# A convolution and gate kernel: more products of zeros at the start, and new orders for the opening and the closing

## The chip, the cores and the metric

The kernel runs on one core of a Trainium2 chip. The metric is the time of one execution on the device in microseconds (us). A core has TensorE (PE, and PEld for its weight loads), VectorE (DVE), ScalarE (ACT), GpSimd (POOL) and SyncE (SP), each with its own stream of instructions, and 16 DMA engines that they share.

## The reference

The input x has shape 8 x 4224 x 192. A causal convolution of seven taps runs along the sequence, with softmaxed weights, one set for each of eight heads of 24 channels. On its result y a gated block is computed: a causal convolution of five taps for each channel, a sigmoid, a product with y times a 192 x 192 matrix, and a second such matrix.

```python
w = exp(weight - max); w = w / (sum(w) + 1e-9)
y[b, s, h, g] = sum over k of w[h, k] * x_pad[b, s + k, h, g]
gate_pre[b, s, d] = sum over k of conv_w[k, d] * y_pad[b, s + k, d]
out = (sigmoid(gate_pre) * (y @ w_val)) @ w_out
```

## The kernel before

**Groups and steps.** The sequences lie one behind the other in two halves, the halves side by side on the partitions. They are cut into nine groups, and each group into four steps (the last into two), 34 in all, of 360 to 512 positions. The 192 channels are in three units: units 0 and 1 (tile x1, one for each half) and unit 2 (tile x2, the remaining 64 channels of both halves).

**First convolution.** `load_x` (token L) fetches a piece of x in windows, on SP's queue, into one of nine buffers. `conv_begin` (U) multiplies a set of windows by the tile `band`, which holds the softmaxed weights: in group 0 a set is 32 matmuls of 64 x 64 by 58 in f32, in the next seven groups 36. A group has six sets. Each needs two loads and two PSUM banks. `conv_end` (K) copies one bank to a tile e on ScalarE, and `scatter` (D) spreads e by DMA over x1 or x2. The eight pieces of group 0's x2 are issued by POOL (`BY_POOL`), all others by SP. Group 0's first two sets give x2, the other four x1.

**Steps.** For step n and unit i, `tap0` (Z) is ScalarE's first tap into PSUM, `tap` (T) one of four multiply-adds on VectorE, `sigmoid` (S) is ScalarE's. `cast_x` (CX, ScalarE) and `rest_x` (XL, GpSimd) split x1 or x2 into a rounded part and a remainder. The tokens V12, V21, V22, V110 and V111 are parts of the product with w_val on TensorE. `gated` (G, VectorE) multiplies it by the gate. `cast_g` and `rest_g` (CG, GL) split that, the parts O12 to O111 are the product with w_out, `evacuate` (E, ScalarE) copies it out of PSUM, and ST stores it. In the last step GL is VectorE's, and E0 too.

**Weights and zeros.** `hw`, `rwv` and `rwo` fetch the head weights and the two matrices, which come as 64-bit numbers. The steps wa, wb, wc (`decode_a`, `decode_b`, `decode_c`) turn a matrix into f32 on VectorE, wp puts it in place (wv on VectorE, wo on GpSimd), wh (`cast`, ScalarE) and wl (`rest`, VectorE) split it. mx, we, sm, bd0 and bd1 make `band`. tl and tl2 load ScalarE's tables. `warm_up` (wu) multiplies a tile of zeros by itself ten times into a bank nothing reads.

**Order.** Nothing is reordered by a scheduler: each engine executes its instructions in the order in which the tokens are written. `PROLOGUE` covers the opening, up to step 4 and parts of step 5. The loop over `window(n)` emits `SCHEDULE` for steps 5 to 17 in pairs. `EPILOGUE` covers the rest, from about step 18 to step 33, with parts of steps 15 to 17. In the token `T21.0` the unit is 2, the tap 1 and the step 0; `D0.0.5` is group 0, x1, head 5; `O110.33` is the product with w_out of unit 0 by its own rows, for step 33.

```python
with tc.manual_schedule(engines={ENG.SP, ENG.PE, ENG.Activation, ENG.DVE, ENG.Pool}):
    emit(PROLOGUE)
    for n in range(FIRST, BEHIND, 2):
        window(n)
    emit(EPILOGUE)
```

Of the kernel before, what the change touches and what calls it, by code (L numbers as in the profile page):

```python
# [112 lines left out]
L T04.0 D1.0.3 Z1.1 XL1.0 G2.1 Z0.1 G2.0 K T11.1 U K T01.1 D1.1.3 T12.1 V21.0 K D1.1.1 T02.1 K
D1.0.1 V111.0 T13.1 CG2.0 D1.1.2 V110.0 S0.0 T03.1 D1.0.2 T14.1 U CG2.1 D1.0.5 T04.1 GL2.1 Z2.2
D1.0.4 U G0.0 Z1.2 L G1.0 GL2.0 K D1.1.0 V111.1 T21.2 K T11.2 CG0.0 U D1.0.7 S0.1 T22.2 T12.2 K
V12.3 CG1.0 T23.2 CX1.2 V21.1 T13.2 GL1.0 T24.2 K V110.1 GL0.0 T14.2 D1.1.7 Z2.3 G1.1 D1.0.6 Z0.2
T21.3 O21.0 K L T01.2 K D1.1.4 V12.2 CG1.1 T22.3 D1.1.5 S2.2 T02.2 O22.0 L CX2.3 T23.3 L O110.0
XL2.3 L T03.2 O12.0 L T24.3 XL1.2 D1.1.6 T04.2 V22.3 Z0.3 G0.1 O111.0 S2.3 T01.3 CX2.2 E1.0 G2.3
# [9 lines left out]
O111.16 T22.19 CX1.18 O22.16 T01.18 CX1.19 XL1.18 O111.15 T23.19 CX2.19 T02.18 V22.18 E2.16 T24.19  # L128
O21.16 K G2.18 Z0.19 XL1.19 O21.15 D6.0.1 T03.18 E1.16 L U T01.19 S2.19 L CG2.17 T04.18 E1.15
O110.16 L T02.19 GL2.17 Z1.19 O110.15 T03.19 S0.18 V111.18 XL2.19 T11.19 E0.15 T04.19 V21.18 E0.16  # L130
ST.15 T12.19 Z1.20 L U G1.18 ST.16 CG0.17 T13.19 K V110.18 GL0.17 CG2.18 T11.20 D6.0.2 K O12.17
T14.19 CG1.17 GL2.18 V12.19 T12.20 Z2.20 G0.18 K GL1.17 V22.19 T21.20 CG0.18 D6.1.2 O22.17 T13.20 K
D6.0.3 GL0.18 O111.17 S0.19 T22.20 L V111.19 D6.1.0 G2.19 CX2.20 V110.19 T23.20 L CX1.20 D6.1.3
T14.20 V21.19 E2.17 D6.1.1 XL1.20 T24.20 O21.17 Z2.21 G1.19 Z0.20 U T21.21 CX1.21 G0.19 O110.17
XL2.20 L E1.17 T22.21 CX2.21 T01.20 V22.20 K XL1.21 T23.21 K O12.18 CG1.18 T02.20 CG1.19 V12.20
T24.21 S2.20 T03.20 V12.21 XL2.21 Z0.21 T04.20 S2.21 V22.21 E0.17 GL1.19 T01.21 O22.18 CG0.19 ST.17
G2.21 Z1.21 O110.18 L GL1.18 T02.21 E2.18 V111.20 G2.20 S0.20 O111.18 T11.21 CG2.19 T03.21 O21.18
GL2.19 T12.21 V21.20 E1.18 T04.21 E0.18 U GL0.19 G1.20 Z1.22 T13.21 V110.20 K L T11.22 D6.0.5 K U
T14.21 CG2.20 ST.18 G0.20 D6.0.4 GL2.20 Z2.22 O22.19 T12.22 L K D6.0.6 T21.22 CG0.20 O12.19 D6.0.7 K
T13.22 O12.20 L E2.19 T22.22 D6.1.4 S0.21 U T14.22 L CX2.22 T23.22 Z2.23 O111.19 XL2.22 D6.1.6  # L140
T24.22 CG1.20 V110.21 T21.23 K O22.20 GL1.20 D6.1.7 Z0.22 T22.23 V111.21 E2.20 L T01.22 GL0.20 S2.22
V21.21 T23.23 K D6.1.5 O21.19 T02.22 CX2.23 O21.20 CX1.22 T24.23 D7.0.0 T03.22 O110.19 Z0.23 XL1.22
G1.21 O111.20 E1.19 T04.22 E0.19 O110.20 E1.20 T01.23 ST.19 Z1.23 V12.22 D7.0.1 G0.21 XL2.23 CG2.21
# [5 lines left out]
CX1.25 T01.24 O21.21 D7.0.4 XL2.25 T24.25 D7.1.1 O22.22 E1.21 T02.24 L CG2.23 O110.21 GL1.22 D7.1.3
Z0.25 T03.24 V22.24 S2.25 T01.25 V110.24 K XL1.25 T04.24 CG0.23 O111.22 E0.21 T02.25 E2.22 V21.24  # L150
ST.21 G2.24 Z1.25 L O21.22 T03.25 GL0.23 CX2.26 D7.0.5 T11.25 U CG2.24 L S0.24 T04.25 GL2.23 V111.24
T12.25 Z1.26 G0.24 O110.22 K T11.26 E1.22 V22.25 D7.0.6 E0.22 T13.25 O12.23 K G1.24 CX1.26 D7.0.7
# [584 lines left out]
```

## Time and profile before

| | us |
|---|---|
| median of three runs | 366.04 |
| lowest, highest | 364.3, 367.31 |
| the profiled execution | 365.04 |
| its span, first to last instruction | 363.2 |

A group's row in the profile names the line, the engine, the operation, what it writes and reads, the shape and the count; behind the bar stand busy time, mean duration in ns, and the idle time of the engine just before, with what ended it. A row of the timeline gives start, duration, engine, line, operation and tiles; the bracket holds the idle time before it and its releaser ("issue" where no semaphore event explains it). A row of stretches gives, for each engine, busy time and number of instructions, then the granted share of TensorE's clock, the DMA share and GB/s. An f32 matmul shows as two rows of TensorE, a rounded one (fp32r) as one, and each row has a weight load.

### The profile page before, as it was taken

The page shows a single profiled execution, that of the slowest core. Times are in us where ns is not written, and L with a number is a line of the kernel's source. Part 1 is how long each engine was busy: PE and PEld are TensorE (multiplying, and loading weights), DVE is VectorE, ACT ScalarE, POOL GpSimd, SP SyncE. Part 2 cuts the span into 40 slices and gives each one's busy share as a digit, 9 for nine tenths or more (in the row PEclk, how much of TensorE's full clock was granted, in tenths as well). Part 3 has the DMA queues.
Part 4 walks back from the last instruction along what each step waited for, and adds up shares of the span by engine and source line. Part 5 has one row for each costly group of instructions (what it writes and reads, how often), then busy time and mean ns, then how long its engine had stood idle before and what let it go on. Part 6 is the DMA issues. An engine that isn't in the chain of part 4 may idle for free.

```text
span 363.2 us, 12709 instructions
## 1 busy us (share of the span) xinstructions
PE 341.8 (94%) x5184; PEld 247.0 (68%) x5184; DVE 338.7 (93%) x551; ACT 318.5 (88%) x550; POOL 242.0 (67%) x191
## 2 busy tenths in 40 slices
...
PEclk9655999999999999999999999999999999999998
...
GB/s 241 338 213 312 227 251 287 152 298 332 212 302 270 221 250 285 263 247 203 275 240 257 269 213 372 183 246 226 250 167 244 257 141 134 110 103 178 36 180 178
DMA packets 36234, 83.21 MB, mean 229 GB/s; under 512 B 4688, under 2 KB 7760, under 8 KB 36176
## 3 DMA queue, kind: packets, MB, share of 16 engines
...
q0 software_dynamic: 384, 0.95, 1.2%
q8 instruction: 41, 0.67, 0.8%
...
## 4 chain that ended last, share of the span: by engine, by line
PE 72%; DVE 13%; DMA 7%; issue 4%; ACT 3%; SPq 0%; DVEq 0%; ACTq 0%
PE pc L386 13%; PE po L553 11%; PE pv L553 11%; DVE pg L468 8%; PE po L536 7%; PE pv L536 7%; PE po L545 7%; PE pv L545 6%; PE po L561 5%; PE pv L561 5%; DMA x<-e 4%; DVE g L583 3%; DMA x<-xw 2%; DVE g L468 2%; ACT e L412 1%
## 5 line engine op out<-in xcount | busy, mean ns | idle before, releaser
L468 DVE SCALAR_TENSOR_TENSOR pg<-x,cwt,pg 128x512 f32<-128x512 f32 (+5 forms) x306 | 210.9, 732 | 4.4 <-ACT pg L458 3.9
L493 POOL TENSOR_TENSOR pl<-g,ph 128x512 fp32r<-128x512 f32 (+4 forms) x99 | 124.1, 1270 | 44.1 <-ACT ph L490 23.2
L493 POOL TENSOR_TENSOR xl<-x,xh 128x1024 fp32r<-128x1024 f32 (+8 forms) x68 | 111.8, 1661 | 54.4 <-ACT xh L490 28.9
L458 ACT ACTIVATE pg<-x,cwt 128x510 f32<-128x510 f32 (+5 forms) x102 | 70.5, 695 | 13.1 <-DVE g L468 8.6
L386 PEld LDWEIGHTS pc<-band,x 64*64 64x64 f32 x3600 | 61.3, 142 | 23.2 <-issue 12.8
L386 PE MATMUL pc<-band,x 64*64 64x58 f32 (+2 forms) x3600 | 67.0, 228 | 9.4 <-issue 8.0
L468 DVE SCALAR_TENSOR_TENSOR g<-x,cwt,pg 128x510 f32<-128x510 f32 (+5 forms) x102 | 73.3, 723 | 0.2
L583 DVE TENSOR_TENSOR g<-pv,g 128x512 f32<-128x512 f32 (+5 forms) x102 | 67.6, 667 | 2.1 <-ACT g L475 1.3
L412 ACT COPY e<-pc 128x512 f32<-128x512 f32 (+2 forms) x102 | 57.6, 591 | 11.6 <-PE pc L386 11.3
L490 ACT CAST ph<-g 128x512 fp32r<-128x512 f32 (+5 forms) x102 | 62.7, 622 | 1.2 <-PE po L545 0.6
L594 ACT COPY ot<-po 128x512 f32<-128x512 f32 (+5 forms) x101 | 56.7, 585 | 5.7 <-ACT g L475 2.3
L475 ACT ACTIVATE g<-g 128x512 f32<-128x512 f32 (+6 forms) x68 | 56.8, 836 | 2.8 <-DVE g L468 2.8
L490 ACT CAST xh<-x 128x512 fp32r<-128x512 f32 (+9 forms) x68 | 54.4, 828 | 0.1
L536 PE MATMUL pv<-x,wvf 128*64 128x256 f32 (+5 forms) x272 | 35.0, 391 | 2.3 <-DMA x<-e 2.3
L536 PE MATMUL po<-g,wof 128*64 128x256 f32 (+5 forms) x272 | 35.5, 384 | 0.0
L553 PE MATMUL pv<-xh,wvh 128*128 128x512 f32 (+5 forms) x68 | 29.3, 431 | 0.1
L536 PEld LDWEIGHTS pv<-x,wvf 128*64 128x64 f32 x272 | 19.2, 142 | 14.4 <-DMA x<-e 2.8
L553 PE MATMUL po<-ph,woh 128*128 128x510 f32 (+5 forms) x68 | 28.1, 413 | 0.5 <-ACT e L412 0.5
L553 PE MATMUL pv<-xl,wvh 128*128 128x512 f32 (+5 forms) x68 | 26.3, 386 | 0.4 <-POOL xl L493 0.4
L553 PE MATMUL pv<-xh,wvl 128*128 128x512 f32 (+5 forms) x68 | 26.2, 386 | 0.1
L553 PE MATMUL po<-ph,wol 128*128 128x510 f32 (+5 forms) x68 | 26.2, 386 | 0.0
L553 PE MATMUL po<-pl,woh 128*128 128x510 f32 (+5 forms) x68 | 26.2, 385 | 0.0
...
## 6 DMA issues: line engine op xcount, KB each, us to landing
x<-xw SPq DMA_DIRECT2D x60, 256.0 KB, 5.6
x<-e SPq DMA_DIRECT2D x56, 256.0 KB, 5.1
...
x<-e SPq DMA_DIRECT2D x8, 232.0 KB, 6.3
...
```

The source lines that it names most:

```text
L386: nc.tensor.matmul(b[r][cols, k * p.run + a : k * p.run + a + n], lhsT=t[rows, o + 64 * c : o + 64 * c + 64], rhs=band[rows, pairs[k] + (c ...
L412: nc.scalar.copy(e[:, :n], opened[g, u][r][:, :n])
L458: nc.scalar.mul(acc, unit_view(n, i, 0), cwt[:, i // 2, 0:1])
L468: nc.vector.scalar_tensor_tensor(out=dst, in0=unit_view(n, i, k), scalar=cwt[:, i // 2, k : k + 1], in1=acc, op0=ALU.mult, op1=ALU.add,)
L475: nc.scalar.activation(v, v, AF.Sigmoid)
L490: nc.scalar.copy(h, x)
L493: eng.tensor_tensor(out=l, in0=x, in1=h.bitcast(F32), op=ALU.subtract)
L536: nc.tensor.matmul(acc[p, c], lhsT=self.w.f[:, W12 : W12 + 64], rhs=self.x1[:, q, c], start=first and i == 0, stop=not first and i == 1,)
L545: nc.tensor.matmul(acc, lhsT=a[p, W21 : W21 + 128], rhs=b[p], start=first and i == 0, stop=not first and i == 2,)
L553: nc.tensor.matmul(acc, lhsT=a[:, W11 : W11 + 128], rhs=b[:, q], start=first and i == 0, stop=not first and i == 2,)
L583: nc.vector.tensor_tensor(out=v, in0=pvs.pop((n, q)), in1=v, op=ALU.mult)
L594: nc.scalar.copy(dst, pos.pop((n, q)))
```

## The change

The zeros are given in two kinds: `warm_up` can first run products on quarters of the array (64 x 64 by 58, four side by side, in two banks), then whole ones of 122 x 122. The first step runs ten rounds of quarters (40 products) and five whole ones, instead of ten whole ones. Steps wx0 to wx3 of four whole products each are added, of which the opening list uses three. The two lists are written in another order; the loop's table is the same. All lines behind `warm_up` have numbers higher by six.

```diff
-    def warm_up(n):
+    def warm_up(n, quarters=0):
 
-        t = bank("warm")
+        t = [bank(f"warm{r}") for r in range(1 + (quarters > 0))]
+        for _ in range(quarters):
+            for r, rows in enumerate(HALVES):
+                for cols in HALVES:
+                    nc.tensor.matmul(
+                        t[r][cols, :WIN], lhsT=zeros[rows, :64], rhs=zeros[rows, :WIN], start=True, stop=True
+                    )
         for _ in range(n):
-            nc.tensor.matmul(t[:122, :122], lhsT=zeros, rhs=zeros, start=True, stop=True)
+            nc.tensor.matmul(t[0][:122, :122], lhsT=zeros, rhs=zeros, start=True, stop=True)
...
 PROLOGUE = """
-hw tl msk wu rwv L L mx L L we L sm L L bd0 bd1 rwo wav L wbv L U U K L K L tl2 U L L K L wao K
+hw tl msk wu rwv L rwo mx L L we L tl2 sm L L L wx0 L wx2 wao L wx1 bd0 bd1 wbo U wav wbv U K L wcv
...
 EPILOGUE = """
...
-ST.32 O12.33 GL1.33 O110.33 E2.33 O111.33 ST2.33 E0.33 E1.33 ST0.33 ST1.33
+ST.32 O12.33 GL1.33 O21.33 E2.33 ST2.33 O111.33 E0.33 ST0.33 E1.33 ST1.33
...
-        "wu": lambda: warm_up(10), "wu2": lambda: warm_up(6), "tl": warm_exp, "msk": band_mask, "mx": maxima, "sm": sums, "L": load_x, "U": conv_begin, "K": conv_end,
+        "wu": lambda: warm_up(5, 10), "tl": warm_exp, "msk": band_mask, "mx": maxima, "sm": sums, "L": load_x, "U": conv_begin, "K": conv_end,
...
+    for i in range(4):
+        ONCE[f"wx{i}"] = lambda: warm_up(4)
```

In the opening, rwo is now the third transfer on SP's queue instead of the tenth, the first two decoding instructions of wo stand ahead of bd0 and bd1 on VectorE, and tl2 stands ahead of the first copies of e on ScalarE.

TensorE at the start of the program, before: the zeros, then the first set of group 0 (pc is its PSUM bank, x the loaded piece; the repeats between are left out).

```order
L725 UNCONDITIONAL_BRANCH
L295 MATMUL warm<-zeros 122x122 x10
L386 MATMUL pc_0_0_170<-band,x_0_137 64x58 x2
L386 MATMUL pc_0_1_171<-band,x_0_137 64x58 x2
L386 MATMUL pc_0_0_170<-band,x_0_139 64x58 x2
L386 MATMUL pc_0_1_171<-band,x_0_139 64x58 x2
```

TensorE at the same place now; the first two rows stand ten times, in turn.

```order
L297 MATMUL warm_125<-zeros 64x58 x2
L297 MATMUL warm_126<-zeros 64x58 x2
L301 MATMUL warm_125<-zeros 122x122 x5
L301 MATMUL warm_197<-zeros 122x122 x4
L301 MATMUL warm_204<-zeros 122x122 x4
L301 MATMUL warm_213<-zeros 122x122 x4
L392 MATMUL pc_0_0_222<-band,x_0_173 64x58 x2
L392 MATMUL pc_0_1_223<-band,x_0_173 64x58 x2
```

All 57 products of zeros stand ahead of the first convolution matmul, where ten did.

SP's queue around group 0's pieces of x1, before (x_0_238 is x1; rows that read `xw` are loads of x).

```order
L244 DMA x_5_283<-xw 128x512
L244 DMA x_0_285<-xw 128x640
L244 DMA x_0_289<-xw 128x512
L430 DMA x_0_238<-e_3_0_428 16x8x464
L430 DMA x_0_238<-e_2_1_301 16x8x464
L430 DMA x_0_238<-e_3_1_430 16x8x464
L430 DMA x_0_238<-e_4_1_474 16x8x464
L430 DMA x_0_238<-e_5_0_478 16x8x464
L430 DMA x_0_238<-e_4_0_433 16x8x464
L430 DMA x_0_238<-e_2_0_296 16x8x464
L430 DMA x_0_238<-e_5_1_496 16x8x464
L244 DMA x_1_508<-xw 128x640
```

SP's queue there now (x_0_294 is x1).

```order
L244 DMA x_5_346<-xw 128x512
L436 DMA x_0_294<-e_2_1_404 16x8x464
L436 DMA x_0_294<-e_3_1_444 16x8x464
L436 DMA x_0_294<-e_2_0_402 16x8x464
L436 DMA x_0_294<-e_4_1_489 16x8x464
L436 DMA x_0_294<-e_4_0_486 16x8x464
L244 DMA x_0_495<-xw 128x640
L244 DMA x_0_498<-xw 128x512
L436 DMA x_0_294<-e_3_0_441 16x8x464
L436 DMA x_0_294<-e_5_1_510 16x8x464
L436 DMA x_0_294<-e_5_0_504 16x8x464
L244 DMA x_1_527<-xw 128x640
```

The first two loads of group 1 moved from ahead of the eight pieces to behind the fifth.

TensorE at the end of the program, before: products with w_out for steps 32 and 33 (po is the bank, ph and pl the split gate product).

```order
L536 MATMUL po_2_5724<-g_32_5571,wof 64x208 x4
L545 MATMUL po_0_5754<-ph_33_5720,woh 128x360
L545 MATMUL po_1_5755<-ph_33_5720,woh 128x360
L545 MATMUL po_0_5754<-ph_33_5720,wol 128x360
L545 MATMUL po_1_5755<-ph_33_5720,wol 128x360
L545 MATMUL po_0_5754<-pl_33_5721,woh 128x360
L545 MATMUL po_1_5755<-pl_33_5721,woh 128x360
L536 MATMUL po_2_5738<-g_33_5639,wof 64x180 x4
L553 MATMUL po_0_5754<-ph_5751,woh 128x360
L553 MATMUL po_0_5754<-ph_5751,wol 128x360
L553 MATMUL po_0_5754<-pl_5752,woh 128x360
```

TensorE at the end now.

```order
L559 MATMUL po_0_5807<-ph_5798,woh 128x360
L559 MATMUL po_0_5807<-ph_5798,wol 128x360
L559 MATMUL po_0_5807<-pl_5799,woh 128x360
L542 MATMUL po_2_5801<-g_33_5683,wof 64x180 x4
L551 MATMUL po_0_5807<-ph_33_5746,woh 128x360
L551 MATMUL po_1_5818<-ph_33_5746,woh 128x360
L551 MATMUL po_0_5807<-ph_33_5746,wol 128x360
L551 MATMUL po_1_5818<-ph_33_5746,wol 128x360
L551 MATMUL po_0_5807<-pl_33_5747,woh 128x360
L551 MATMUL po_1_5818<-pl_33_5747,woh 128x360
```

For step 33, O110 (the rows that read ph_5798 and pl_5799) moved from behind O21 and O12 to ahead of both; in both programs three more rows follow, O111.

More of the change, by code (lines that the diff above doesn't have):

```diff
@@ L113 @@
[L113 to L118, printed above, removed]
@@ L124 @@
+L G1.2 V21.3 L E2.1 T12.4 GL2.2 L K U K T21.4 S0.3 XL2.4 T13.4 D2.1.1 V12.4 D2.0.2 T22.4 CG0.2 T14.4
+V110.3 T23.4 Z2.5 O12.2 G0.3 CG1.2 V111.3 T24.4 GL1.2 T21.5 Z0.4 G1.3 GL0.2 S2.4 K K D2.0.4 L L
+D2.0.1 D2.0.5 D2.0.3 L D2.0.0 L D2.1.3 D2.1.2 D2.1.0
 """
@@ L127 @@
 EPILOGUE = """
[L128 to L143, printed above, removed]
@@ L149 @@
[L149 to L152, printed above, removed]
-V12.25 T12.26 CG1.23 T14.25 U GL1.23 G2.25 Z2.26 T13.26 O22.23 K T21.26 GL2.24 CG0.24 D7.1.6 U
-T14.26 E2.23 ST.22 K XL2.26 T22.26 L V21.25 Z2.27 D7.1.4 T23.26 O21.23 K XL1.26 D7.1.7 S0.25 T21.27
@@ L179 @@
[L179 to L182 removed]
+T22.19 CX2.19 O21.16 K XL2.19 T23.19 CX1.18 O111.15 T01.18 D6.0.1 V22.18 CX1.19 T24.19 L XL1.18
+O22.16 T02.18 Z0.19 O110.15 T03.18 E2.16 O110.16 CG0.17 T01.19 O111.16 S2.19 GL0.17 T04.18 E0.16
@@ new lines @@
+O12.20 T23.23 L V12.23 CG0.20 T01.22 D7.0.0 S2.22 T24.23 GL0.20 K O21.20 T02.22 CX2.23 D7.0.1 O22.20
+Z0.23 G2.22 XL2.23 O110.19 T03.22 CG2.22 V22.23 T01.23 E2.20 GL2.22 S2.23 O110.20 T04.22 O111.19
+T02.23 XL1.23 Z1.23 O111.20 G2.23 CG0.21 T11.23 E0.20 V110.22 S0.22 T03.23 V111.22 T12.23 E1.20
+O21.19 T04.23 CG1.21 V21.22 E0.19 T13.23 GL1.21 Z1.24 U G0.22 CG2.21 T14.23 GL0.21 E1.19 V111.23
+T11.24 K ST.19 Z2.24 G1.22 GL2.21 V21.23 ST.20 S0.23 T12.24 U T21.24 CX2.24 G1.23 CX1.24 O12.21
+XL2.24 T13.24 K T22.24 V110.23 K XL1.24 D7.0.3 T14.24 O22.21 K D7.0.2 CX2.25 G0.23 O111.21 D7.1.3
@@ new lines @@
+T11.26 Z2.27 O22.23 XL1.26 T12.26 CX2.27 V110.25 E2.23 T21.27 V111.25 K T13.26 S0.25 D7.1.7 U T22.27
+D7.0.7 CX1.27 T14.26 O110.23 D7.1.6 G0.25 Z0.26 D7.1.4 V22.26 G1.25 CG0.24 D7.0.6 T01.26 O21.23
+CG1.24 L S2.26 T23.27 GL1.24 D7.1.5 O111.23 K T02.26 O22.24 D8.0.0 CG1.25 T24.27 GL0.24 V12.27
+T03.26 Z0.27 V12.26 XL2.27 T04.26 E1.23 K T01.27 O12.24 Z1.27 D8.0.1 GL1.25 T02.27 S0.26 V22.27
+T11.27 O110.24 E0.23 G2.26 E2.24 ST.23 O12.25 T12.27 S2.27 D8.0.2 CG0.25 T03.27 L O21.24 CG2.25
+T13.27 D8.0.3 V21.26 GL2.25 E0.24 T04.27 O111.24 G2.27 Z1.28 XL1.27 T14.27 V110.26 E1.24 T11.28
```

93 lines of the change are left out of this document (52 added, 41 removed).

## The prediction

> **What bounds the kernel now.** I read the page first: busy shares, the clock in the slices, the queues.
>
> ```profile
> span 363.2 us, 12709 instructions
> ...
> PE 341.8 (94%) x5184; PEld 247.0 (68%) x5184; DVE 338.7 (93%) x551; ACT 318.5 (88%) x550; POOL 242.0 (67%) x191
> ...
> PEclk9655999999999999999999999999999999999998
> ...
> q8 instruction: 41, 0.67, 0.8%
> ```
>
> Two engines are nearly full and TensorE ran at half clock early on. One queue carries instructions: 41 packets for TensorE's 5184 + 5184 = 10368 instructions, so 253 a packet. Next, busy time by stretch, cut where TensorE stops.
>
> ```profile
> 0.00:10.60 10.60, 8.71 (x222) 7.90 (x222) 3.05 (x15) 5.00 (x10) 1.63 (x12) 1.00 0.78 265
> 10.60:13.60 3.00, 0.11 (x5) 0.00 (x0) 2.35 (x6) 0.97 (x3) 3.00 (x6) 0.81 1.06 396
> 13.60:17.32 3.72, 3.68 (x127) 3.50 (x127) 3.51 (x11) 0.92 (x3) 1.13 (x3) 0.50 1.07 283
> 20.30:24.01 3.71, 3.66 (x127) 3.50 (x127) 0.56 (x1) 1.38 (x3) 0.83 (x3) 0.50 0.97 207
> ...
> 45.95:100.00 54.05, 53.02 (x772) 37.86 (x772) 53.68 (x86) 49.85 (x87) 34.80 (x26) 1.00 0.93 256
> 100.00:300.00 200.00, 199.04 (x3119) 142.33 (x3122) 198.88 (x307) 191.83 (x327) 149.04 (x105) 1.00 0.82 244
> 300.00:354.90 54.90, 54.36 (x426) 38.45 (x418) 54.32 (x90) 49.09 (x88) 42.09 (x32) 1.00 0.34 128
> ```
>
> Columns: TensorE matmuls, TensorE loads, VectorE, ScalarE, GpSimd, then clock, DMA share, GB/s. From 45.95 to 354.9 VectorE idles 0.37 + 1.12 + 0.58 = 2.1 us in 309. It sets the pace there, and a new order cannot give back more than that 2.1 us. What can be won lies before 46 us and after 354.9. The counts show the other limit: TensorE stops after 444 instructions, then after 254 more, then 254 again, about the 253 of one packet. The stops are waits for a read of instructions.
>
> ```profile
> 1.15 4.49 PE L295 MATMUL warm<-zeros 128*122 128x122 f32 x20 [1.15 <-DVE zeros L299]
> 13.64 3.68 PE L386 MATMUL pc<-band,x 64*64 64x58 f32 x127 [2.93 <-issue]
> 20.35 3.66 PE L386 MATMUL pc<-band,x 64*64 64x58 f32 x127 [3.04 <-issue]
> 25.97 0.75 PE L561 MATMUL pv<-xh,wvh 128*128 128x462 f32 x1 [1.96 <-ACT xh L490]
> 45.97 0.45 PE L386 MATMUL pc<-band,x 64*64 64x58 f32 x15 [1.32 <-issue]
> ```
>
> "issue" means that no semaphore explains the wait. From go-on to go-on: 20.35 - 13.64 = 6.7 us and 25.97 - 20.35 = 5.6 us for one packet's worth, of which the work is 3.7. Last, what VectorE waits for, and the transfers behind it:
>
> ```profile
> 10.54 4.19 POOL L430 DMA_DIRECT2D x<-e  x8 [8.10 <-ACT e L412]
> 11.18 0.36 DVE L307 TENSOR_SCALAR wo_g<-raw_wo 128x384 int32<-128x384 int32 x1 [5.32 <-DMA raw_wo<-wo]
> 15.33 0.98 DVE L338 TENSOR_TENSOR wvf<-wv_h,wv_l 128x64 f32<-128x64 f32 x5
> 17.39 8.78 SPq L430 DMA_DIRECT2D x<-e  x8
> 23.59 1.22 ACT L458 ACTIVATE pg<-x,cwt 128x464 f32<-128x464 f32 x2 [0.45 <-DMA x<-e]
> 31.33 1.22 ACT L458 ACTIVATE pg<-x,cwt 128x464 f32<-128x464 f32 x2 [3.04 <-DMA x<-e]
> 32.02 3.75 DVE L468 SCALAR_TENSOR_TENSOR pg<-x,cwt,pg 128x464 f32<-128x464 f32 x6 [2.27 <-ACT pg L458]
> 37.88 1.19 DVE L583 TENSOR_TENSOR g<-pv,g 128x462 f32<-128x462 f32 x2 [0.90 <-ACT g L475]
> 39.77 2.52 DVE L468 SCALAR_TENSOR_TENSOR pg<-x,cwt,pg 128x462 f32<-128x462 f32 x4 [0.71 <-ACT pg L458]
> ```
>
> VectorE's work on group 0 starts in earnest at 32.02, when the last of eight pieces of x1 has landed (31.33, where ScalarE's first tap goes on) plus 0.69 of that tap. After it come two waits, 0.90 + 0.71 = 1.6 us, and then it is full. So the time is: landing of x1, plus those waits, plus fixed VectorE work, plus the tail.
>
> **The change part by part.**
>
> *Zeros.* Ten products of zeros were 20 matmul rows in 4.49 us, 0.224 a row. Now there are 40 quarter products (80 rows) and 5 + 12 whole ones (34 rows). A quarter product has the shape of a convolution matmul: at half clock 127 rows in 3.68, 0.029 a row, so 2.3 us. The five: 10 x 0.224 = 2.2, to 1.15 + 4.5 = 5.7 us, about where the old zeros ended. The last 24 rows take 24 x 0.224 = 5.4 at that price and about 2.7 if the clock has doubled. TensorE reaches group 0 at 8.4 (or 11.1) where it was there at 5.6. I take 8.4: in the trace the clock reads 1.00 in the first row and the zeros before it were as dense. What covers the delay: the band now stands behind the decode of raw_wo, and nothing can start before it; with raw_wo issued ahead of the second load, it should be there near 7.6 (estimate).
>
> *Where the reads fall.* Each f32 matmul is four instructions (10 zeros, 20 rows, as many weight loads). Before, the first stop lies (444 - 40) / 4 = 101 convolution matmuls in, the next at 164.5 and 228. Now 57 products of zeros are 228 instructions: stops at (444 - 228) / 4 = 54, 117.5, 181, 244.5. Group 0 has 6 x 32 = 192, so three stops fall inside it where two did. I take the first to be covered: its read, asked for one packet ahead, is asked for among the zeros, by 5.7, and at 5.6 to 6.7 us a read it is there at 11.3 to 12.4, while TensorE gets there at 8.4 + 54 x 0.037 = 10.4 (67.0 us for 1800 convolution matmuls in the page's group, shown next). Price 0 to 2 us, taken at 0.5, since the DMA engines are less loaded at 3 us than at 13.6.
>
> ```profile
> L386 PE MATMUL pc<-band,x 64*64 64x58 f32 (+2 forms) x3600 | 67.0, 228 | 9.4 <-issue 8.0
> ...
> x<-xw SPq DMA_DIRECT2D x60, 256.0 KB, 5.6
> ...
> x<-e SPq DMA_DIRECT2D x8, 232.0 KB, 6.3
> ...
> x<-e POOLq DMA_DIRECT2D x8, 116.0 KB, 8.7
> ```
>
> The second stop comes near 13 and lasts to about 17, the third ends near 23, and the last 11 matmuls of group 0 end near 23.4. Before, they ended at 20.35 + 27.5 x 0.058 = 21.9. So TensorE itself is 1.5 us later, not earlier. What can make x1 earlier is the rest.
>
> [...] Here the first stop comes after 444 and costs 2.93 us. [...]
>
> *VectorE and ScalarE.* raw_wo is third in SP's queue, so VectorE no longer waits 5.32 us for it with wv's decode behind it. wvf was done at 15.33 + 0.98 = 16.3; now about 13.5 (7.6, then the same decode instructions: two of wo, four and five of wv at 0.36 to 0.57, and the 0.98). ScalarE's cast of wvh, which the copies behind it wait for, comes 2.8 us earlier, and with it SP's first piece of x1 (17.39, now 15).
>
> *SP.* Two loads of group 1 move from ahead of the eight pieces to behind the fifth.
>
> ```profile
> 0.00:31.33 31.33, 19.21 (x482) 16.52 (x482) 16.92 (x45) 12.94 (x25) 9.97 (x26) 0.70 0.93 268
> 14.50:23.59 9.09, 6.05 (x228) 5.87 (x223) 5.20 (x15) 3.26 (x8) 2.13 (x6) 0.50 1.05 226
> ```
>
> The DMA engines are full (share 0.93) up to x1's landing: 268 GB/s x 31.33 us = 8.4 MB. What x1 needs is 12 loads of 0.26, the two weights (0.78), eight pieces of 0.116 and eight of 0.232: 6.6 MB; with the two loads still ahead of its last pieces, 7.2 MB, or 27.0 us at that rate. That is the early end. The late end is 31.33 plus the 1.5 us by which TensorE is later: 32.8. I take 29.4, nearer the middle: the pieces start 2.4 us earlier, but the last needs TensorE at 23.4, a copy, and the 6.3 us that such a piece takes to land. Gain 1.9, between +1.5 and -4.3.
>
> *VectorE's later waits.* The first gate product is now step 0's, whose sigmoid is early, so the 0.90 goes; late next is TensorE, whose stop after 1458 instructions falls in step 1's products. I give it the 1.32 of the stop at 45.97: 1.6 becomes 1.3. Ends 0 and 2.5.
>
> *The middle and the closing list.* The loop's code is the same, its read boundaries shift. One wait of VectorE in 300 us came from TensorE (0.7, below); I take one again, between none and three. The closing list keeps the end: last taps, sigmoid, two gate products, two remainders on VectorE, then TensorE's last 24 matmul rows.
>
> ```profile
> DVE g L583 <- PE pv L545: 0.7, 1, 0.7
> ...
> 356.12 0.53 DVE L493 TENSOR_TENSOR pl<-g,ph 128x360 fp32r<-128x360 f32 x1 [0.22 <-ACT ph L490]
> 357.11 0.53 DVE L493 TENSOR_TENSOR pl<-g,ph 128x360 fp32r<-128x360 f32 x1 [0.45 <-ACT ph L490]
> ...
> 357.51 0.43 PE L553 MATMUL po<-ph,woh 128*128 128x360 f32 x1
> ```
>
> O110.33 now starts once the first remainder is there (356.65), with O12 and O21 behind it, about 1.5 us of cover for the second (357.64). It ends within 0.3 of before: 0.
>
> *Sum.* -1.9 - 0.3 + 0 + 0 = -2.2 us. The profiled execution was 365.04 (span 363.2 and 1.8 around it), which gives 362.8. The median of the runs is 366.04, 1.0 above it; on that the forecast is **363.8 us**.
>
> **Rivals.** *First, slower: the clock comes late.* If the clock has not doubled by 5.7, the zeros last to 11.1, group 0 starts 2.7 later than forecast, and x1 lands at 32.8 or later: 31.33 + 1.5 + 2.7 less what the DMA queue hides, about 34. That is +2.7 less 0.3: 368.4. It decides from a start of group 0 after about 10. For it: the row at 10.60 to 13.60 shows 0.81, the clock does fall. Against: 4.5 us of zeros sufficed once. [...] *Second: all falls into place.* x1 lands near 27 and both later waits go: -4.3 - 1.0 = -5.3, 360.7. For it: 1.2 MB of other loads were moved before x1 landed. Against: the last piece needs TensorE. *Third: no effect.* x1 lands when the DMA engines are done, at 31.3 as now, and the stops were covered by that wait: 366.0. For it: DMA share 0.93 to 1.06 all the way. *Fourth: the closing list costs VectorE.* It is full there, and four waits like the 0.7 above add 2.8: 366.6.
>
> **How the numbers follow.** Forecast 0.40, first 0.12, second 0.21, third 0.21, fourth 0.06. The forecast's own range is 362 to 365.5. For 8 in 10 the range goes from 360.4 (the second rival) to 367.9 (most of the first). A measurement of this kernel can tell about 1% from no change, that is 362.4 and 369.7. Faster: the second rival nearly whole (0.18) and a quarter of the forecast (0.10), 0.28. Slower: a third of the first and a part of the fourth, 0.07. The same: 0.65.
>
> **What would show it.** Counts by stretch: the first stop within group 0 absent or short, stops after 698 and 952 instructions of about 3 us. Zeros to 8.4, the clock at 1.00 by 6. ScalarE's first tap on x1 at 29.4 instead of 31.33, VectorE's idle time after it about 1.3 us. If x1 lands at 31 or later, or if VectorE idles over 2 us between 100 and 355, the forecast is wrong.

## The result, and the profile after

The changed kernel takes 370.40 us (median of 5 runs, 369.81 to 371.25) against 366.04 us before: a ratio of 1.0124, with a 95% interval from 1.008 to 1.0169. It is slower: both ends of the interval lie above 1. The profiled execution took 371.25 us, 6.2 more than the one before (365.04). In a second session the medians were 370.12 and 365.11 us (ratio 1.0098, 1.0042 to 1.0154).

Single executions of one kernel lie up to 9 us apart here, and the ratios use those within 1.5% of a kernel's fastest; a long wait for instructions stands in the profile of one of the others, as will be seen.

From the page of the profile after, the same rows as were shown of the page before:

```profile
span 369.3 us, 12883 instructions
...
PE 345.9 (94%) x5278; PEld 248.7 (67%) x5278; DVE 339.8 (92%) x551; ACT 319.0 (86%) x550; POOL 242.4 (66%) x191
...
PEclk9865999999998999999999999999999999999999
...
q8 instruction: 41, 0.67, 0.8%
```

VectorE's work is 339.8 us where it was 338.7, so some 5 of the 6.1 us of span are waits of VectorE; the other 1.1 us are longer instructions of its own, for which no run here shows a reason. Where the waits lie is told by its busy time by stretch; the columns are start and end, length, VectorE's busy time (instructions), granted clock, DMA share, GB/s. Before:

```profile
33.00:60.00 27.00, 25.02 (x43) 0.94 0.90 254
60.00:100.00 40.00, 40.00 (x64) 1.00 0.91 252
100.00:115.00 15.00, 15.00 (x25) 1.00 0.94 287
115.00:354.00 239.00, 237.70 (x373) 1.00 0.70 214
```

After:

```profile
33.00:60.00 27.00, 24.39 (x41) 0.90 1.05 261
60.00:100.00 40.00, 39.69 (x63) 1.00 0.89 242
100.00:115.00 15.00, 10.90 (x18) 0.89 1.01 280
115.00:354.00 239.00, 237.95 (x369) 1.00 0.70 214
```

Idle time went from 1.98 to 2.61 us in the first stretch, from 0 to 0.31 in the second, from 0 to 4.10 in the third, and from 1.30 to 1.05 in the rest: +4.8 us, of which one stretch of 15 us has 4.1. The clock there is 0.89. Ahead of 33 us VectorE idles 15.99 us where it was 15.10, and behind 354 us 5.49 where it was 6.13. The timelines of TensorE, SyncE, ScalarE and VectorE in the opening:

```profile
14.92 3.53 PE L392 MATMUL pc<-band,x 64*64 64x58 f32 x127 [2.17 <-issue]
19.55 0.57 PE L392 MATMUL pc<-band,x 64*64 64x58 f32 x22 [1.10 <-issue]
26.11 1.34 PE L392 MATMUL pc<-band,x 64*64 64x58 f32 x40 [5.99 <-DMA x<-xw]
...
19.77 1.03 SPq L244 DMA_DIRECT2D x<-xw  x2
20.85 2.70 SPq L436 DMA_DIRECT2D x<-e  x3
...
32.29 1.22 ACT L464 ACTIVATE pg<-x,cwt 128x464 f32<-128x464 f32 x2 [7.79 <-DMA x<-xw]
...
32.97 3.75 DVE L474 SCALAR_TENSOR_TENSOR pg<-x,cwt,pg 128x464 f32<-128x464 f32 x6 [6.28 <-DMA x<-xw]
```

The zeros did their work: only two stops of 2.17 and 1.10 us are left inside group 0, and its last product ends at 19.55 + 0.57 = 20.1 us. Yet VectorE's first tap on x1 starts at 32.97, 0.95 later than before: TensorE was early, and the transfers were not.

The largest loss, seen on the timelines of TensorE and, in the last row, of VectorE near 106 us:

```profile
103.02 2.31 PE L392 MATMUL pc<-band,x 64*64 64x58 f32 x144
105.26 1.08 PE L542 MATMUL po<-g,wof 128*64 128x254 f32 x8
109.07 0.50 PE L559 MATMUL pv<-xh,wvh 128*128 128x510 f32 x1 [2.73 <-DVE pg L474]
...
110.73 0.63 PE L559 MATMUL pv<-xh,wvh 128*128 128x510 f32 x1
...
113.90 0.69 DVE L589 TENSOR_TENSOR g<-pv,g 128x510 f32<-128x510 f32 x1 [4.10 <-PE pv L551]
```

Two neighbouring sets of convolution products (144 rows, with their loads 288 instructions) take 2.3 us; after eight rows of another product comes a gap of 2.73 us. The row behind it names VectorE's tap as the releaser, but the gap is a wait for instructions, as the next two views show. First, TensorE's rows in the 3 us ahead of the gap, in the gap and behind it (products, loads, VectorE, ScalarE, GpSimd, clock, DMA share, GB/s):

```profile
103.37:106.35 2.98, 2.98 (x144) 2.32 (x136) 2.98 (x5) 2.98 (x7) 2.52 (x2) 1.00 1.06 316
106.35:109.07 2.72, 0.00 (x0) 0.00 (x0) 2.72 (x6) 2.72 (x6) 2.33 (x2) 1.00 1.01 395
109.07:113.75 4.68, 4.68 (x19) 2.90 (x19) 0.73 (x2) 1.97 (x4) 3.97 (x4) 0.64 0.93 295
```

Second, the queues of the transfers in 106.5 to 107.7 us (from 103.37 to 106.5 the view has no row for the queue of instructions at all):

```profile
q1 hardware_dynamic: 94, 0.47, 98.5%
q8 instruction: 1, 0.02, 5.7%
```

So TensorE used up a block of 256 instructions (the prediction worked out 253 for a packet) in 2.98 us, the read of the next began 3.1 us after the block was entered, ran 1.1 us, and TensorE went on another 1.4 us later. Behind the gap the clock is granted at 0.64 for 4.7 us, and VectorE, whose next gate product waits for TensorE, loses 4.1 us for a gap of 2.7.

### The profile page after: what moved, and what is told of

Read it like the earlier page. It is cut to its first block, busy times and chain, and to the rows that moved or that the text cites. A ratio compares the mean times of both kernels' runs of the same rounds, so it can differ in the third digit from the quotient of the medians.

```text
span 369.3 us, 12883 instructions
## 1 busy us (share of the span) xinstructions
PE 345.9 (94%) x5278; PEld 248.7 (67%) x5278; DVE 339.8 (92%) x551; ACT 319.0 (86%) x550; POOL 242.4 (66%) x191
## 4 chain that ended last, share of the span: by engine, by line
PE 82%; DMA 10%; DVE 3%; issue 2%; ACT 1%; POOL 0%; SPq 0%; DVEq 0%; ACTq 0%
PE pc L392 14%; PE pv L559 13%; PE po L559 12%; PE po L542 8%; PE pv L542 8%; PE po L551 7%; PE pv L551 7%; PE po L567 6%; PE pv L567 6%; DMA x<-xw 6%; DMA x<-e 5%; DVE pg L474 2%; PE warm L301 1%; ACT e L418 1%; PE warm L297 1%
## 5 line engine op out<-in xcount | busy, mean ns | idle before, releaser
L499 POOL TENSOR_TENSOR xl<-x,xh 128x512 fp32r<-128x512 f32 (+7 forms) x68 | 112.2, 1663 | 68.3 <-ACT xh L496 21.6
L600 ACT COPY ot<-po 128x512 f32<-128x512 f32 (+5 forms) x101 | 57.6, 584 | 10.7 <-ACT g L481 2.9
L496 ACT CAST xh<-x 128x512 fp32r<-128x512 f32 (+7 forms) x68 | 55.2, 836 | 2.6 <-PE pv L551 2.6
```

What stands on the lines that cost most here:

```text
L496: nc.scalar.copy(h, x)
L499: eng.tensor_tensor(out=l, in0=x, in1=h.bitcast(F32), op=ALU.subtract)
L600: nc.scalar.copy(dst, pos.pop((n, q)))
```

## The experiments

Block boundaries can be counted. Number TensorE's recorded instructions from 0, its waits for semaphores and its three drains included: in every profile here the stops of this kind stand ahead of numbers 449, 705, 961 and so on, every 256th (in the kernel before at 13.63, 20.35 and 25.97 us; the gap that ends at 109.07 in the changed one stands ahead of 3777, which is 449 + 13 x 256). So instructions that are added ahead of a place, where TensorE idles anyway, move the boundaries there and are meant to move nothing else. All medians in one table (runs of one session share the runs of the kernel before; its medians were 365.1 to 366.3):

| run | from | median us (lowest to highest, runs) | ratio to before (95%) |
|---|---|---|---|
| e2_old_closing | changed | 370.33 (367.88 to 375.86, 6) | 1.0116 (1.0071 to 1.0161) |
| b_new_zeros | before | 365.07 (362.58 to 371.05, 10) | 0.9971 (0.9927 to 1.0014) |
| e4_old_zeros | changed | 374.30 (372.74 to 377.51, 4) | 1.0280 (1.0202 to 1.0359) |
| e3_loads_last | changed | 374.45 (373.38 to 379.31, 4) | 1.0250 (1.0202 to 1.0297) |
| e6_loads_first | changed | 373.60 (370.23 to 376.76, 6) | 1.0169 (1.0105 to 1.0233) |
| e1_pad128 | changed | 369.57 (367.47 to 371.68, 4) | 1.0126 (1.0066 to 1.0185) |
| e5_pad_late | changed | 375.73 (373.88 to 377.83, 4) | 1.0296 (1.0209 to 1.0382) |
| b_pad208 | before | 367.19 (366.39 to 371.20, 10) | 1.0062 (1.0013 to 1.0110) |
| b_pad64 | before | 369.42 (366.73 to 369.57, 4) | 1.0104 (1.0024 to 1.0184) |
| a_split | changed | 370.91 (369.00 to 374.66, 6) | 1.0130 (1.0071 to 1.0189) |
| bz_split | before | 366.47 (365.55 to 368.67, 12) | 1.0036 (1.0011 to 1.0061) |
| after_again | changed | 370.12 (365.24 to 374.41, 10) | 1.0098 (1.0042 to 1.0154) |
| b_new_zeros2 | before | 364.73 (363.60 to 366.56, 10) | 1.0009 (0.9978 to 1.0039) |
| e8_no_stores | changed | 365.84 (362.71 to 368.19, 10) | 1.0030 (0.9993 to 1.0068) |
| a_no_wx | changed | 364.77 (363.31 to 369.38, 12) | 0.9993 (0.9958 to 1.0029) |
| c_quarters | before | 364.41 (362.03 to 371.18, 12) | 0.9981 (0.9941 to 1.0020) |

**Which part of the change costs.** The closing list was put back:

```diff
 EPILOGUE = """
-T22.19 CX2.19 O21.16 K XL2.19 T23.19 CX1.18 O111.15 T01.18 D6.0.1 V22.18 CX1.19 T24.19 L XL1.18
+O111.16 T22.19 CX1.18 O22.16 T01.18 CX1.19 XL1.18 O111.15 T23.19 CX2.19 T02.18 V22.18 E2.16 T24.19
...
```

> The changed kernel with the closing list of before; opening list and zeros as changed. Theory (the closing list costs and gives nothing; the loss lies before 115 us): 369.5 to 371.5, the stop at 106 and VectorE's 4.0 us there as in the changed kernel. Rival (the closing list gives VectorE new waits): 366 to 368.

It took 370.33 us, with a gap of 1.59 us at 108.7 in the profiled execution (368.11), smaller than expected there: the closing list costs and gives nothing that shows. Then the zeros alone were put into the kernel before:

```diff
-hw tl msk wu rwv L L mx L L we L sm L L bd0 bd1 rwo wav L wbv L U U K L K L tl2 U L L K L wao K
+hw tl msk wu rwv L L mx L L we L sm L wx0 wx2 L wx1 bd0 bd1 rwo wav L wbv L U U K L K L tl2 U L L K L wao K
...
-        "wu": lambda: warm_up(10), "wu2": lambda: warm_up(6), "tl": warm_exp, "msk": band_mask, "mx": maxima, "sm": sums, "L": load_x, "U": conv_begin, "K": conv_end,
+        "wu": lambda: warm_up(5, 10), "tl": warm_exp, "msk": band_mask, "mx": maxima, "sm": sums, "L": load_x, "U": conv_begin, "K": conv_end,
```

> The kernel before with the changed kernel's zeros alone (first zeros in quarters and three steps of four more), its lists as before; 188 instructions more ahead of group 0. If the zeros do what they are for: no stop at the first boundary within group 0, short ones at the next two, its last product ends 1 to 2 us earlier than 24.0 and x1 lands at 29.5 to 31 instead of 31.3. The boundaries behind it move by 188: blocks nearly wholly in pairs end near 47, 104 (2.9 us of work) and 201 (2.0); stops of 1 to 3.5 us there, VectorE idle 1 to 3 us behind each of the last two. Time 365.5 to 370. Rival (zeros alone carry the change's worth, and the moved boundaries cost nothing): 363 to 365.

365.07 us, just between the two that were expected: no loss, no sure gain. The first stop of group 0 is gone, and VectorE's first tap on x1 starts at 31.44 instead of 32.02. Against e2_old_closing, which differs from it in the opening list alone, that is 5.3 us, so the loss came with the opening list. But the execution that was profiled here was a long one, 371.05 us, and its timeline has the same gap:

```profile
108.08 0.79 PE L559 MATMUL pv<-xh,wvh 128*128 128x510 f32 x1 [4.25 <-DVE pg L474]
```

The two kernels have the same boundary there, so the old list too can lose time at it. The other way round, the zeros of before in the changed lists:

```diff
-hw tl msk wu rwv L rwo mx L L we L tl2 sm L L L wx0 L wx2 wao L wx1 bd0 bd1 wbo U wav wbv U K L wcv
+hw tl msk wu rwv L rwo mx L L we L tl2 sm L L L L wao L bd0 bd1 wbo U wav wbv U K L wcv
...
-        "wu": lambda: warm_up(5, 10),
+        "wu": lambda: warm_up(10),
```

> The changed kernel's lists with the zeros of before: ten whole products, none in quarters, none of the three later steps; 188 instructions fewer ahead of group 0. If the zeros are what brings the reads of instructions forward: the first stop of 2.9 us is back inside group 0's 192 products, and group 0's last product ends at 21.5 to 23 instead of 20.1. If the landing of x1 hangs on that: it lands at 33.5 or later, time over 371; if it hangs on the queue of transfers alone: at 31.5 to 32.5, and the time is set by the blocks, which begin 188 instructions later in the code: the block near 105 still lies mostly in the pair of sets (stop of 1 to 2.5 us), time 368.5 to 371.

The first stop was back in group 0, as expected (2.52 us, with a second of 2.24), the last product of group 0 ended at 19.7 us, earlier than the 21.5 to 23 expected, and VectorE's first tap on x1 began at 32.07, so x1 did not hang on the zeros. The time, 374.30 us, was above what was expected: other blocks had stops,

```profile
88.27 1.89 PE L392 MATMUL pc<-band,x 64*64 64x58 f32 x68 [1.77 <-issue]
105.58 0.61 PE L392 MATMUL pc<-band,x 64*64 64x58 f32 x26 [0.93 <-issue]
...
243.33 0.33 PE L392 MATMUL pc<-band,x 64*64 64x48 f32 x7 [1.60 <-issue]
```

so, by this one profile, the zeros were worth more in the changed lists for where they put the boundaries than for anything they did early on.

**SyncE's two loads.** They were moved behind the last piece of x1, and in another run ahead of the first:

```diff
-D0.0.3 wpo U K D0.0.0 K D0.0.5 who D0.0.4 wlo L wlv L Z2.0 D0.0.2 T21.0 K CX2.0 T22.0 K XL2.0 T23.0
-CX2.1 D0.0.7 Z2.1 T24.0 D0.0.6 XL2.1 T21.1 S2.0
+D0.0.3 wpo U K D0.0.0 K D0.0.5 who D0.0.4 wlo wlv Z2.0 D0.0.2 T21.0 K CX2.0 T22.0 K XL2.0 T23.0
+CX2.1 D0.0.7 Z2.1 T24.0 D0.0.6 L L XL2.1 T21.1 S2.0
```

> The changed kernel with the two loads of group 1 moved on SP's queue from behind the fifth to behind the eighth piece of x1. Theory (x1 lands late because these two loads, 2.7 us in the queue, go ahead of its last three pieces): the last piece lands at 29 to 30 us instead of 32.26, VectorE's first tap on x1 starts at 30 to 31 instead of 32.97, the rest as before, time 367.5 to 369. Rival (the pieces themselves go slowly, at 150 GB/s, whatever stands ahead of them): the last lands at 31.5 to 32.5, time 370 to 371.

VectorE's first tap on x1 came 3.1 us earlier, as the theory had it, and the time rose by 4 us, which it had not. TensorE's and VectorE's timelines:

```profile
31.08 2.17 PE L392 MATMUL pc<-band,x 64*64 64x58 f32 x72 [8.63 <-DMA x<-xw]
...
29.90 3.75 DVE L474 SCALAR_TENSOR_TENSOR pg<-x,cwt,pg 128x464 f32<-128x464 f32 x6 [0.72 <-ACT pg L464]
...
41.05 3.73 DVE L474 SCALAR_TENSOR_TENSOR pg<-x,cwt,pg 128x462 f32<-128x462 f32 x6 [4.95 <-ACT pg L464]
```

Group 1's first set waits 8.63 us for its loads, and VectorE waits 4.95 us at 41, in the first taps of group 1: the queue's order says which of the two is late.

```diff
-K L U K L K D0.1.6 U D0.1.0
+K L U K L K L L D0.1.6 U D0.1.0
...
-D0.0.3 wpo U K D0.0.0 K D0.0.5 who D0.0.4 wlo L wlv L Z2.0
+D0.0.3 wpo U K D0.0.0 K D0.0.5 who D0.0.4 wlo wlv Z2.0
```

> The changed kernel with the two loads of group 1 ahead of all eight pieces of x1 on SP's queue, as the kernel before has them. Theory (the queue of transfers sets the landing of x1, and having the loads in the middle of the pieces only makes group 1's first set late): the loads land by 19 us, TensorE's wait of 5.9 us ahead of group 1's first set goes, the last piece lands at 30.5 to 32; VectorE's waits from 33 to 60 us fall from 2.6 to under 2 us; the stop near 106 stays; time 369 to 370.4. Rival (pieces land later behind two more loads): last piece at 33 or later, 371 or more.

The wait of 5.9 us went and VectorE's first tap on x1 began at 32.49, as the theory had it; the time rose to 373.60. The profiled execution, the longest of six, had longer stops (4.02 us at 23.36, 3.22 at 40.67, 2.25 at 54.76, 2.52 at 113.52). Neither place of these two loads wins back the loss.

**Moving the boundaries.** 128 instructions of zeros were put where TensorE idles:

```diff
+    ONCE["wy"] = lambda: warm_up(0, 8)
...
-CX2.1 D0.0.7 Z2.1 T24.0 D0.0.6 XL2.1 T21.1 S2.0 L L T22.1 L U T23.1
+CX2.1 D0.0.7 Z2.1 T24.0 D0.0.6 XL2.1 T21.1 S2.0 L L T22.1 L wy U T23.1
```

> The changed kernel with 32 quarter products of zeros more, 128 instructions, put where TensorE idles from 20.1 to 26.0 us, ahead of group 1's first set: every later block of 256 instructions begins 128 instructions earlier in the code, and nothing else moves. Theory (a stop comes where one block lies wholly inside two neighbouring sets of convolution products, 288 instructions that TensorE works off in 2.3 us): the block that was used up in 2.97 us and left TensorE idle for 2.73 us at 106.3 is now half other products, so VectorE's idle 4.0 us at 109.8 goes; other blocks (near 42, 85, 187, 227 and 285 us) take its place in such pairs and may cost 0 to 1.5 us. Time 366 to 368.5 against 370.4. Rival (the read came late at that time because the DMA engines are loaded there, whatever the block holds): a stop of 2 to 3 us stays between 100 and 112, time 370 to 371.

The gap at 106 is gone (VectorE is busy 15.00 of 15.00 us from 100 to 115), but the time is 369.57 us, above the 366 to 368.5 expected: two other blocks have stops, the first far above the 1.5 us that were expected,

```profile
44.42 0.45 PE L392 MATMUL pc<-band,x 64*64 64x58 f32 x16 [3.24 <-issue]
88.82 0.32 PE L392 MATMUL pc<-band,x 64*64 64x48 f32 x3 [1.49 <-issue]
```

The rival, a read that is slow at that time whatever the block, falls; so does the hope that the replaced stops are small. A padding of as many instructions at 62 us, of smaller products, so that the opening keeps its boundaries:

```diff
+    def fill(n):
+        t = bank("fill")
+        for j in range(n):
+            cols = HALVES[j % 2]
+            nc.tensor.matmul(t[cols, :16], lhsT=zeros[:64, :64], rhs=zeros[:64, :16], start=True, stop=True)
...
-Z1.4 O12.1 G2.3
+Z1.4 wy O12.1 G2.3
```

> The changed kernel with 32 small products of zeros (128 instructions, one extra bank) put in at about 62.7 us, ahead of step 1's product O12, where TensorE idles 0.93 us; everything ahead of it, the block boundaries too, stays as in the changed kernel, and from there on each block begins 128 instructions earlier in the code. Theory (the 4 us at 106 come from a block that lies wholly in a pair of convolution sets): no stop over 1 us at 103 to 112, VectorE's idle time from 60 to 115 us falls from 4.4 to 0.5 to 1.7 us (a boundary now falls into the pair at 87 us, where the first shift had a stop of 1.49 and 1.0 us of VectorE), time 366.5 to 368.5. Rival (something else in the changed list makes VectorE wait there): 370 to 371.

Again no gap at 106, and again one at the pair that took its place, 3.46 us at 90.1 (clock 0.91 over 80 to 100 us). But the padding itself cost VectorE 3.5 us at 68.6 and so the time, 375.73 us, says nothing on the theory. The same kind of padding in the kernel before, of 52 and of 16 products (one place for both):

```diff
-T24.0 L T22.1 S2.0 V22.0 L T23.1
+T24.0 L T22.1 S2.0 V22.0 wy L T23.1
```

> The kernel before with 52 small products of zeros (208 instructions) put in at about 27 us, where TensorE waits for x1; lists and first zeros as before. Blocks that lie wholly in a pair of convolution sets now end near 47, 103 and 201 us (2.6, 2.0 and 2.0 us of work each). Theory (a read is started only 2 to 3.5 us after TensorE enters the block ahead, takes 1.1 and 1.4 more until TensorE goes on): stops of 2 to 4 us near 47, 103 and 201, VectorE idle 1.5 to 3.5 us behind each of the last two, time 368.5 to 372 against 365.4. Rival (the lists cost, not the place of the boundaries): 365 to 366.5.

> The same with 16 small products (64 instructions). Blocks wholly in a pair end near 39, 64, 83 and 181 us. Theory: stops of 1 to 4 us at two or more of them, time 367 to 371. Rival: 365 to 366.5.

With 64 instructions it came as expected: stops of 1.53, 1.26, 1.25 and 2.00 us at 39.6, 50.2, 85.0 and 183.7 (none at 64), and 369.42 us, from 16 small products of zeros where TensorE waits. With 208 it did not: the stop at the pair near 106 was 0.85 us, at 201 there was none, and 367.19 us, 0.6% above before, lies under the 368.5 to 372 expected. There VectorE waits 6.25 us from 33 to 60 us and 0.77 from 100 to 115. Whether a block lies in a pair can be counted; how late its read starts cannot.

Then the pair of sets was parted in the loop, in the changed kernel and in the one before with the new zeros:

```diff
-G0-1 GL0-2 U T14+0 CX2+1 K T11+1 GL2-2 Z2+1 O12-2 G1-1 CG1-2 T12+1 V111+0 S0+0 GL1-2 T21+1
+G0-1 GL0-2 T14+0 CX2+1 K T11+1 GL2-2 Z2+1 O12-2 G1-1 CG1-2 T12+1 V111+0 U S0+0 GL1-2 T21+1
```

> The changed kernel with one set of the loop moved: in SCHEDULE the second of two neighbouring U goes behind V111+0, so that 22 slower instructions (1.7 us of other products) stand between the two sets; number of instructions and everything ahead of the loop as before. Theory (the 4 us at 106 come from a block that lies wholly in a pair of sets and is used up in 2.97 us): that block now lasts about 4.4 us, the stop at 103 to 110 falls from 2.73 to 1.3 us or less, the clock stays at 1.00 there, VectorE's idle time from 100 to 115 us falls from 4.1 to under 1.5 us; time 367 to 368.5 against 370.4. Rival (the read is simply slow at that time, or the list makes VectorE wait there anyway): idle 3 us or more there, 370 to 371.5.

> The kernel before with the changed kernel's zeros (as in the run with the zeros alone) and the moved set of the loop. Theory: the block boundaries are as in the run with the zeros alone, where the stop at 103.8 lasted 4.2 us in the profiled execution; with the pair split it lasts under 2.5 us, no execution is over 368, the median is 363.5 to 365. Rival (the executions of 370 had another cause): some executions over 369, median 365 to 366.

The block at 106 behaved as the theory had it. From a_split, a row of TensorE's timeline and VectorE's row by stretch:

```profile
106.61 0.32 PE L392 MATMUL pc<-band,x 64*64 64x48 f32 x3 [0.64 <-issue]
...
100.00:115.00 15.00, 13.92 (x22) 1.00 0.95 285
```

The medians did not: 370.91 and 366.47 us, the second no better than with the pair. In a_split the profiled execution was the shortest of six, 369.00, so its profile does not tell what the others lost. Even its span, 367.0, is 3.8 us above before, half of it VectorE's longer instructions (340.6 us of work for 338.7) and half waits in many places, 1.08 us of them from 100 to 115. So a gap at one block can be mended while the kernel gains nothing, and the stop at 106 alone does not account for the median.

**Why the read starts late.** The changed kernel without the output's transfers of steps 0 to 19, and two kernels once more:

```diff
-        nc.sync.dma_start(out[:, AT[n] + a * m : AT[n] + b * m], ots[n][0][:, a * m : b * m])
+        if n >= 20:
+            nc.sync.dma_start(out[:, AT[n] + a * m : AT[n] + b * m], ots[n][0][:, a * m : b * m])
```

> The changed kernel without the output's transfers of steps 0 to 19 (their results are computed and not stored). It tells whether a read of instructions starts late because the DMA engines are loaded: the mean DMA share from 60 to 200 us falls from about 0.9 to 0.6. If so: the stop at 106 falls from 2.73 to under 1 us, that at 90 from 0.73 to 0, VectorE's idle from 60 to 115 us from 4.4 to under 1.5 us, time 365.5 to 368. Rival (a read starts late whatever the load): stops as before within 0.5 us, 369.5 to 371.

> The changed kernel once more, for a second profiled execution. If the stop at 106 us belongs to the kernel (the block, and a read that starts about 3 us after TensorE enters it): a stop of 1.5 to 3 us there again, VectorE idle 1.4 to 4 us behind it, x1's last piece at 31 to 32.5, time 369 to 371. If it was the chance of one execution: stop under 0.7 us there and a time about as before it, 370, made of other waits.

> The kernel before with the new zeros alone once more, for the profile of an execution near its median of 365.07 (the profiled one was 371.05, with a stop of 4.24 us at 103.8 and VectorE idle 6.2 us behind it). Theory: in an execution of 363 to 366 the same block is entered, but its read starts within 1 us, the stop is under 1 us and VectorE's idle from 100 to 115 us under 1.2 us. Rival: the stop is there all the same and the 6 us came from elsewhere.

In all three the same block is used up in 2.97 or 2.98 us. From e8_no_stores, the block and its gap in the columns that TensorE's block had above, and the queue of instructions from 102.64 to 103.65 us:

```profile
102.03:105.00 2.97, 2.97 (x144) 2.32 (x136) 2.97 (x6) 2.97 (x7) 2.52 (x2) 1.00 0.16 52
105.00:105.14 0.14, 0.01 (x2) 0.00 (x1) 0.14 (x1) 0.14 (x2) 0.04 (x1) 1.00 0.15 29
...
q8 instruction: 1, 0.02, 6.0%
```

The DMA engines were loaded to 0.16 there instead of 1.06, the read began 0.6 us after the block was entered instead of 3.1, the gap is 0.14 us, and from 60 to 200 us VectorE idles 0.80 us (139.20 of 140.00) instead of 4.48. The time, 365.84 us, is as expected, but with fewer transfers it is not that of a kernel that does the same work. In after_again and b_new_zeros2, block and gap:

```profile
102.77:105.75 2.98, 2.98 (x144) 2.32 (x136) 2.98 (x6) 2.98 (x7) 2.53 (x2) 1.00 1.08 291
105.75:109.38 3.63, 0.00 (x0) 0.00 (x1) 3.63 (x6) 3.50 (x7) 3.08 (x3) 1.00 0.97 373
...
102.11:105.08 2.97, 2.97 (x144) 2.31 (x136) 2.97 (x6) 2.97 (x7) 2.52 (x2) 1.00 1.03 405
105.08:106.56 1.48, 0.00 (x0) 0.00 (x0) 1.48 (x3) 1.48 (x4) 1.27 (x1) 1.00 0.92 325
```

The changed kernel has the gap again, 3.63 us, and the old list with the same zeros has it too, 1.48 us, half a microsecond above what was expected of it; VectorE lost 1.14 us there (13.86 of 15.00). The load of the engines made the read late: 0.6 us after entry at 0.16, 1.9 and more at 1.03 to 1.08. A share over 1 does not say how late: the kernels with this block differ in what the engines move during it. The read began 1.9 us after entry where they moved 405 GB/s (b_new_zeros2) or 396 (e2_old_closing), 3.1 at 316 (the changed kernel), 4.0 at 291 (after_again) and 4.6 at 252 (b_new_zeros): the later, the less they moved. Both lists stand at both ends of this row, so it does not say what the opening list does to it.

**The boundaries moved by 48.** Last, the changed kernel without the three later steps of zeros, 48 instructions, and the kernel before with the quarters only:

```diff
-hw tl msk wu rwv L rwo mx L L we L tl2 sm L L L wx0 L wx2 wao L wx1 bd0 bd1 wbo U wav wbv U K L wcv
+hw tl msk wu rwv L rwo mx L L we L tl2 sm L L L L wao L bd0 bd1 wbo U wav wbv U K L wcv
```

> The changed kernel without its three later steps of zeros (12 products, 48 instructions fewer ahead of group 0, 1.5 us in which TensorE waits for the band anyway). Every block begins 48 instructions later in the code: the one that was used up in 2.97 us at 106 now ends in slower products and lasts over 6 us. Theory: no stop over 0.3 us between 100 and 112 and VectorE idle under 0.5 us there; pairs are hit near 56 and 168 us instead (2.0 us of work each) and near 129 (3.2), where stops of 0 to 3 us cost VectorE 0 to 3 us; time 366 to 369 against 370.1. Rival (the opening list costs its 5 us whatever the boundaries): 369.5 to 371.

> The kernel before with the first zeros in quarters (ten, and five whole) and no later steps; lists as before. Theory: no stop between 100 and 112; pairs near 48, 125 and 164 us with 2.6, 3.1 and 2.0 us of work, where the stops stay under 2 us; time 363.5 to 365.5, few executions over 368. It would be the version to keep if it is faster than both kernels; rival: 365 to 367, no gain.

a_no_wx took 364.77 us, 5.4 less than the changed kernel in the session before, under the 366 to 369 expected, and level with the kernel before (0.9993, 0.9958 to 1.0029). TensorE waits for the band where the zeros were, so that group 0 starts at the same time (7.85 us for 7.78); the block at 106 now ends among slower products (its row, and VectorE's by stretch),

```profile
105.04:111.05 6.01, 6.01 (x155) 4.40 (x151) 6.01 (x10) 6.01 (x12) 5.39 (x5) 1.00 0.93 356
...
100.00:115.00 15.00, 15.00 (x24) 1.00 0.97 290
```

lasts 6.01 us, and VectorE does not wait at all there. Group 0 has one boundary fewer too (stops of 0.19 and 1.75 us), and VectorE's first tap on x1 started at 31.82, within the spread given below. Its profiled execution, one of its longest (367.77), shows the pair that is hit instead, 57.60 after a stop of 4.13 us. On the old lists the same twelve products make no difference (c_quarters 364.41, b_new_zeros 365.07 and 364.73), so there they do not cost time by themselves. c_quarters is the fastest median, but its interval holds 1: none of these is a version that is surely faster than the kernel before.

## Why the prediction was wrong

The forecast was 363.8 us within 360.4 to 367.9; it was 370.4, on the side that had 0.07.

**Zeros and clock: right.** The 34 rows of whole products took 4.37 us, where 20 took 4.49 before; their starts in the trace are 0.21 us apart up to 4.5 us and 0.11 from then on. So the clock had doubled before the 5.7 us that the forecast needed, and the zeros ended at 7.8 us (8.4 forecast). The row that was read for it proves nothing: the granted clock reads 1.00 from 0 us on, also where the products still run at half that pace. The first rival, a late clock, did not happen, though its time (368.4) came nearest: the time came out by another way.

**The reads in group 0: right in kind, too dear.** The first stop was covered; the other two were 2.17 and 1.10 us where about 3 each was put in, so group 0 ended at 20.1, not 23.4. In a_no_wx, 48 instructions fewer ahead of group 0 were worth 5.4 us.

**x1's landing: wrong.** The term took 29.4 us, between 27.0 from bytes at 268 GB/s and a late end of 32.8. It was 32.29. The last three pieces were issued at 20.85 to 23.6, as early as assumed, and took about 9 us to land. The engines were full and slower while they did, from 26.1 to 32.3 us now and from 26.1 to 31.3 before:

```profile
26.10:32.30 6.20, 3.90 (x75) 2.94 (x75) 0.59 (x1) 0.01 (x1) 0.00 (x0) 0.50 1.06 198
...
26.10:31.30 5.20, 2.92 (x6) 1.49 (x6) 3.51 (x6) 1.21 (x3) 2.09 (x2) 0.50 1.05 301
```

Its early end counted 7.2 MB up to the landing, with two loads of group 1. The engines moved 256 GB/s over those 32.29 us, 8.3 MB, about as much as before: other loads were moved while the last pieces were under way. Of the 1.23 MB from 26.1 to 32.3 us, the rows of the pieces (215 packets between 512 B and 2 KB) were only 0.40. With the two loads behind the pieces (e3_loads_last) x1 landed at 29.21, near the forecast, and group 1 paid for it. Why the rate was 198 and not 301 is not shown. How much of the 0.95 us is the change's is less sure: ScalarE's first tap on x1 began between 29.52 and 33.37 in nine profiles with the changed opening list and loads (mean 31.8), and between 29.87 and 32.20 in seven with the old one (mean 30.8), so about 1 us later.

**VectorE's later waits:** 1.3 us forecast from 33 to 60 us, 2.61 measured (1.98 before, in the same view). The stop that was forecast in step 1's products came, but with 0.50 us (39.58) for 1.32. The largest wait, 1.69 us at 52.20, is for TensorE, behind two ends of blocks that were not forecast: stops at 45.98 and 50.65 of 0.76 and 0.48.

**The middle: the step that failed.** "Its read boundaries shift ... I take one again, between none and three" priced a stop in the loop by the one that had been seen, 0.7 us. The boundaries were counted for group 0 and not for the loop, though the same count would have shown that a block now lay almost wholly inside a pair of sets at 106 us. It cost VectorE 4.1 us in this profile and 4.5 in after_again (10.49 of 15.00 us busy), above the upper end of 2.1 for three such waits: the row it was priced by was one short stop, and neither a later read (3.1 us after entry) nor the lower clock behind the gap (0.64 for 4.7 us) was in it. The count alone would not have given the price: the old lists with the new zeros have the same block and lose nothing in the median (365.07 and 364.73). Both signs by which the prediction was to be known as wrong came: x1 landed after 31, and VectorE idled 5.15 us between 100 and 355 (1.73 before).

The terms account for the profiled execution, 6.2 us longer where 2.2 less was forecast: x1's landing is off by 2.9 (0.95 later for 1.9 earlier), the later waits by 0.9, the middle by 4.2 (0.31 + 4.10 - 0.25 for nothing), VectorE's own work by 1.1, and the end gave 0.6 back.

**The closing list: right**, nothing (e2_old_closing).

What stays open: why the changed opening list loses its 5 us in the median at boundaries that the old lists share, at a DMA share over 1 in both; and what the executions of a_split lost that were not profiled. That the stops move with the boundaries, and that the one at 106 goes with the load of the DMA engines, is shown; that this stop makes the whole difference of the medians is not.
